# Two attention blocks on one core: eight value groups moved into the attention loop, the first maxima started among the query projections, a ring of query quarters

## The chip, the cores and the metric

The kernel runs on one core of a Trainium2 chip. TensorE (PE; its weight loads are listed apart as PEld) multiplies, VectorE (DVE) and ScalarE (ACT) read the results out of PSUM, GpSimd (POOL) works in SBUF, and SyncE (SP) issues nearly every DMA. PSUM is used as eight banks of 512 fp32 numbers per partition. The metric is the device time of one execution in microseconds (us); lower is better.

## What is computed

Two independent attention blocks, A and B, each on 2048 rows of width 640 with 32 heads of 20 columns, side by side in the output:

```python
qkv = (x @ wqkv).reshape(B, S, 3, H, Dh)              # both blocks
# A: every row sees 8 rows, 0, 2, ... 14 rows back
logits = einsum("bhsd,bhswd->bhsw", q, kg) * scale
o_a = einsum("bhsw,bhswd->bhsd", softmax(logits), vg)
# B: every row sees every row
p = softmax(einsum("bhqd,bhkd->bhqk", q, k) * scale)
o_b = einsum("bhqk,bhkd->bhqd", p, v)
return concatenate([o_a @ wo_a, o_b @ wo_b], axis=-1)
```

## The kernel before

**Products of x.** Every projection is split into a high and a low part and made of three passes (`PASSES`, L30) over five chunks of 128 rows of the width (`KC`), so one output group is 15 matmuls into one bank. The stages follow each other: A's projections (L530 on), then B's queries and keys, then B's values, then a long loop with B's attention, in which A's attention runs beside on GpSimd, then a tail.

**Queries and keys of B (L594 to L630).** 40 groups of 128 columns of weights by 512 rows of x, in ten weight chunks `MS` (keys first, queries last), two chunks `j` and four row blocks `n` at a time. Each group is copied out by ACT, its remainder is subtracted by DVE (tile `pr`), and both are stored to DRAM (`qb_d`, `kb_d`). In the last eight groups (m == 8) the weights of V's first half are loaded (tile `ww`), and the keys of the first head group (tile `bk`).

**Values of B (L922 to L977).** 32 groups (`v_group`): 16 blocks `s` of 128 rows by two halves of 320 columns; ACT copies each into a tile `ve` and SP stores it to `vb_d`. The last two (`LAG`) are left for the loop's start, so 30 stand here. B's x is held in four tiles `xn` of one rotating set of four buffers ("big"), which the keys `bk` and queries `bq` of the head groups also use; blocks 0 and 1 of x are thrown out for `bk` and `bq` of head group 0 and loaded a second time (L956) for V's last groups. V starts with blocks 2 and 3.

**Maxima.** The softmax of B subtracts each row's maximum before the exponential. The maxima are made by a pass of their own: scores are multiplied once as "m" matmuls (queries stationary, tiles `bq,bk`), and DVE reduces them from PSUM to `mx`. One of 512 such steps (`b_max`, L727) has four matmuls of 60 rows by 512 columns into two pairs of banks (`wide()`), and two DVE reductions over 1024 numbers. The maxima run 24 steps (`LEAD`) ahead of the rest: 24 `b_max` are set one behind each of V's groups 7 to 30. When 16 steps are through, `max_rows` (L636) turns the maximum round, splits it on POOL, and sends it through DRAM (`mdr`) into two extra rows of the query tile, from where the second score matmul subtracts it.

**The loop (L1008 to L1043).** 512 steps in 32 units of 16: eight head groups `g` of four heads, four quarters `qc` of the queries each. Per step: four "s" matmuls (keys stationary, tiles `bk,bq`) whose banks ACT exponentiates (tile `e`), four "m" matmuls of the step 24 ahead whose banks DVE reduces, and eight matmuls of the values (`e,vb`, "P"). The order of a unit is written out by hand:

```python
UNIT = ("P ss MM sm P sm ss MM sm sm P ss MM sm P sm MM ss sm sm P sm MM ss P sm MM ss sm sm P ss MM sm P "
        "sm MM ss sm sm P ss MM sm P sm ss MM ss G sm ss MM sm P sm MM ss P sm MM sm ss P sm MM ss P sm "
        "MM sm ss P MM MM ss P ss MM sm sm").split()          # L847
```

"ss" is a pair of score matmuls, "MM" a pair of maximum matmuls with one reduction of 1024, "sm" one of each with a reduction of 512. "G" (`group`, L1002) is one group of A's output projection (tiles `ww,aot`, 15 matmuls), and behind it the small DVE work that waited in `beside` (`flush`). `one`, `two` and `bank` choose the PSUM banks by a running account of when each was read. `b_two` (L810) issues a pair.

**Beside it.** Every fourth step calls one unit of A's attention (`a_work`), whose POOL work is on tiles `akv`; POOL also adds B's partial sums (`braw<-braw,more`) and splits A's output (`aot`). In the loop's early steps, the keys, queries (20 DMAs) and values of the next head group are loaded at every second step (`b_pieces`, L563, L1013). SP issues in program order, so a DMA that waits holds up those behind it. `after(n, ...)` defers work by n ticks; a tick is one group before the loop and one step in it.

Of the kernel before, what the change touches and what calls it, by code (L numbers as in the profile page):

```python
# [64 lines left out]
def attention_pair(ctx, tc, xa, wqk_a, wv_a, wo_a, xb, wqk_b, wv_b, wo_b, oa, ob):  # L65
# [121 lines left out]
    def columns(n):  # L187

        return (sb.tile([128, 2, KC - 1, 512], F32R, tag="big", bufs=4, name="xn"),
                sb.tile([128, 2, 1, 512], F32R, tag=f"last{n % 4 // 2}", bufs=2, name="xl"))  # L190
# [15 lines left out]
    def wide_pieces(src, second=None):  # L206

        w = [sb.tile([128, KC, 320], F32R, tag="w", bufs=4, name="ww") for _ in range(2)]
        return w, [lambda a=a, b=b: split(
            w[0][:, a:b], w[1][:, a:b], src[:, a:b], second=second, first=second and gp.tensor_copy) for a, b in PAIRS]  # L210
# [53 lines left out]
    def rows15(p, o, W):  # L264

        for k in range(KC):
            for i, (wi, xi) in enumerate(PASSES):
                pe.matmul(p[:, :320], o(xi, k), W[wi][:, k], start=(k == 0 and i == 0), stop=(k == KC - 1 and i == 2))

# [291 lines left out]
    stacks = {}  # L561

    def b_pieces(g):  # L563
        k = sb.tile([128, 2, S], F32R, tag="big", bufs=4, name="bk")
        q = sb.tile([128, NQC, 2, 512], F32R, tag="big", bufs=4, name="bq")
        v = sb.tile([128, NKB, VG], F32, tag="vb", bufs=2, name="vb")
        stacks[g] = (q, k, v)
        out = []
        hs = [slice(g * GH + 2 * r, g * GH + 2 * r + 2) for r in range(2)]

        def add(t, src, runs):
            for r0, s0, n in runs:
                out.append(lambda: sp.dma_start(t[r0:r0 + n].bitcast(F32), src[s0:s0 + n]))
        for r in range(2):
            for r0, s0, n in BK_RUNS:
                add(k[r * HALF:], kb_d[:, hs[r]], [(r0, s0, n)])
        for qc in range(NQC):
            for r in range(2):
                for r0, s0, n in BQ_RUNS:
                    add(q[r * HALF:, qc], qb_d[qc, :, hs[r]], [(r0, s0, n)])  # L580
        return out[:4], out[4:]

    def v_piece(g, b0, b1):

        sp.dma_start(stacks[g][2][:, b0:b1], vb_d[b0 * 128:b1 * 128, g * GH * VC:g * GH * VC + VG]
                     .rearrange("(b p) c -> p b c", p=128))
# [8 lines left out]
    for m in range(0, 10, 2):  # L595
        nxt = []
        for n in range(4):
            for j in range(2):
                p = next(banks)
                for k in range(KC):  # L600
                    for i, (wi, xi) in enumerate(PASSES):
                        pe.matmul(p, WB[j][:, wi, k], chunk(XB[n], xi, k), start=(k == 0 and i == 0),
                                  stop=(k == KC - 1 and i == 2))
                c = MS[m + j]
                o = (0, 1) if c < KC else (1, 0)
                pt = sb.tile([128, 2, 512], F32R, tag="p", bufs=PB, name="pr")
                act.copy(pt[:, o[0]], p)
                dve.tensor_tensor(pt[:, o[1]], p, pt[:, o[0]].bitcast(F32), ALU.subtract)
                after(1, sp.dma_start, dst_b(c, n).rearrange("t p c -> p t c"), pt.bitcast(F32))
                tick()  # L610
                if loads:
                    loads.pop(0)()
                if m < 8 and (n, j) in ((1, 0), (1, 1)):
                    w, loads = m_pieces(MS[m + 2 + len(nxt)])
                    nxt.append(w)
                elif m == 8 and (n, j) == (0, 1):
                    WV, loads = wide_pieces(wv_b[0])
                elif m == 8 and n == 3:
                    if j == 0:
                        wait[0] = 4  # L620
                        w1, more = wide_pieces(wv_b[1])
                        for fn in more:
                            fn()
                if m == 8 and n > 1:
                    if (n, j) == (2, 0):
                        k_loads, q_loads = b_pieces(0)
                    k_loads.pop(0)()
# [80 lines left out]
    def m_matmul(i, j, r, p):  # L708
# [3 lines left out]
        q, k, v = stacks[g]  # L712
# [7 lines left out]
    def max_end(i, n=2):  # L720
# [3 lines left out]
        if left_m[u] == 0:  # L724
            max_rows(*mxt[u], stacks[u // NQC][0], u % NQC)
# [15 lines left out]
    def s_matmul(i, pl, r, p):  # L741
        u, kb = divmod(i, NKB)
        g, qc = divmod(u, NQC)
        q, k, v = stacks[g]
# [26 lines left out]
    def b_pv(i):  # L771
# [15 lines left out]
        for j in range(GH):  # L787
            pe.matmul(acc[32 * j:32 * j + 32, :], stacks[g][2][:, kb, j * VC:j * VC + 32], P[i][j % 2][:, j // 2],
# [21 lines left out]
    def b_two(what):  # L810
# [39 lines left out]
        "MM sm ss P MM MM ss P ss MM sm sm").split()  # L850
    SLOT = UNIT[:UNIT.index("G")].count("P") - 1

    def b_units(pv, group):
# [5 lines left out]
        for i in range(0, NS - LEAD, NKB):  # L859
            for t in UNIT if i + NKB <= NS - LEAD else PAIR * (NKB // 4):  # L860
# [3 lines left out]
                elif t == "G":  # L864
                    group()
                elif t == "ss":
# [20 lines left out]
    def out_first(qc):  # L887

        o = columns(2)
# [32 lines left out]
    steps = iter(range(LEAD))  # L922
    WV = [WV, w1]
    groups = 0

    def v_group(n, half, s):
        p = bank()
        rows15(p, lambda xi, k: chunk(XB[n], xi, k)[:, s % 4 * 128:s % 4 * 128 + 128], WV[half])
        ve = ones[s % 4]
# [5 lines left out]


    WO, loads = [], []

    def load_out(src, W, halves=range(2)):
        for h in halves:  # L940
            w, more = wide_pieces(src[h], gp)
# [3 lines left out]
    V_GROUPS = [(n, half, s) for n in (2, 3, 0, 1) for half in range(2) for s in range(4 * n, 4 * n + 4)]  # L945
    v_late = V_GROUPS[-LAG:]
    for n, half, s in V_GROUPS[:-LAG]:
        v_group(n, half, s)
        tick()
        groups += 1  # L950
        if q_loads:
            for _ in range(4 if groups == 1 else 1):
                q_loads.pop(0)()
        if groups == 1:
            wait[0] = 5
        if groups in (8, 16):  # L956
            XB[groups // 8 - 1], more = x_pieces(xb, groups // 8 - 1, gp)
            for fn in more:
                fn()
        if groups > 6:  # L960
            for i in islice(steps, 1):
                b_max(i)
        if groups in (9, 11, 15, 17, 19, 23, 25, 28):
            next(a_work, None)
        if groups in (26, 28):
            v_piece(0, *((0, 4) if groups == 26 else (8, 16)))
        if groups == 14:
            a_turn(*done_a.pop(0)[1:])
        turn_parts()
        if groups == 28:  # L970
            wait[0] = 2
            load_out(wo_a, WO, (0,))
        if loads and groups >= 28:
# [34 lines left out]
    steps = b_units(lambda i: b_pv(i) if i >= 0 else v_group(*v_late.pop(0)), group)  # L1008
    next(steps)
    for i in range(NS + LAG):  # L1010
        g, sub = divmod(i, NQC * NKB)
        if sub == 4 and g + 1 < NG:
            k_loads, q_loads = b_pieces(g + 1)  # L1013
            for n, fn in enumerate(k_loads + q_loads + [lambda g=g + 1: v_piece(g, 0, NKB)]):
                after(1 + 2 * n, fn)
        if i in (NS - 56, NS - 40):
            out_first((i - NS + 56) // NKB)
# [9 lines left out]
        if i == 1:  # L1027
            load_out(wo_a, WO, (1,))
# [73 lines left out]
```

## Time and profile before

| what | value |
|---|---|
| three timed runs | 1774.38, 1775.05 (median), 1775.96 us |
| the profiled execution's own time | 1773.91 us, of which its span is 1772.1 us |
| TensorE's granted clock | 1.00 throughout |
| queries and keys, last eight groups | about 321.8 to 349.0 us |
| V's 30 groups with the 24 first maxima | about 349.0 to 437.1 us |
| the loop's units 0 to 31 | from 447.7 us (first accumulated sum copied out); about 39.65 us each up to unit 27 |
| units 28 and 29, with two "G" groups each | 41.88 and 41.87 us |

How to read the rows below. A line of the timeline is: start, duration, engine, line (all are L60, a helper that issues everything), operation, output<-inputs, shape, how many instructions were merged, and in brackets the idle time ahead of them with what ended it. A window's line is: stretch, its length, then the busy time of PE, PEld, DVE, ACT and POOL with the number of instructions, the granted clock, and the share and rate of the DMA engines. A line of groups is: tiles, shapes, count, total and mean duration, and idle time before.

### The profile page before, as it was taken

How to read it: one execution, taken by the hardware profiler on the slowest of the kernel's cores; microseconds unless marked ns; L12 is line 12 of the kernel's file. 1: busy time of each engine (PE TensorE's matmuls, PEld its weight loads, DVE VectorE, ACT ScalarE, POOL GpSimd, SP SyncE). 2: the span in 40 equal slices, each digit the busy share in tenths (PEclk: the TensorE clock that was granted, in tenths of full speed). 3: DMA queues.
4: the chain of work that ended last, by engine and by line, in shares of the span. 5: the costliest groups of instructions: out<-in, count | busy, mean ns of one | idle time of the engine just before them, and what ended most of it. 6: DMA issues, size and time to landing. Idle time of an engine off the chain costs nothing.

```text
span 1772.1 us, 31387 instructions
## 1 busy us (share of the span) xinstructions
PE 1761.4 (99%) x11211; PEld 982.3 (55%) x11211; DVE 1332.0 (75%) x1774; ACT 1325.7 (75%) x2593; POOL 1218.8 (69%) x1072
## 2 busy tenths in 40 slices
PE   9999999999999999999999999999999999999999
PEld 8988888888444444444444444444444444444569
DVE  3100232267999999999999999999999999999400
ACT  4222322222999999999999999999999999998981
POOL 0000058448698988989898898989898898745442
PEclk9999999999999999999999999999999999999999
DMA  6333596876443534364444435353543534222123
GB/s 230 112 98 110 175 309 244 278 227 200 121 123 114 138 103 129 115 164 113 129 114 140 119 97 149 123 144 105 156 129 93 143 103 120 87 63 62 57 70 115
DMA packets 191188, 240.20 MB, mean 136 GB/s; under 512 B 89020, under 2 KB 115260, under 8 KB 190040
## 3 DMA queue, kind: packets, MB, share of 16 engines
q1 hardware_dynamic: 190456, 237.54, 44.7%
q8 instruction: 88, 1.44, 0.3%
q14 instruction: 68, 0.56, 0.1%
q10 hardware_dynamic: 576, 0.66, 0.1%
HBM read 173.21 MB, written 64.91 MB: 134 GB/s over the span
## 4 chain that ended last, share of the span: by engine, by line
PE 86%; DVE 5%; ACT 3%; POOL 3%; DMA 1%; issue 1%; SPq 1%; POOLq 0%; DVEq 0%; ACTq 0%
PE ps_st L60 86%; DVE mx L60 5%; ACT e L60 2%; POOL akv L60 1%; ACT more L60 1%; POOL braw L60 1%; SPq L60 1%; DMA bq<-qb_d 1%; DMA stg<-wv_b 0%; ACT al L60 0%; DMA back<-tr_d 0%; POOL aot L60 0%; DMA tr_d<-turn 0%; POOL al L60 0%; POOL ao L60 0%
## 5 line engine op out<-in xcount | busy, mean ns | idle before, releaser
L60 DVE TENSOR_REDUCE mx<-ps_st 128x2 f32<-128x1024 f32 (+1 forms) x1452 | 1204.3, 901 | 53.6 <-PE ps_st L60 50.6
L60 ACT ACTIVATE e<-ps_st 128x512 f32<-128x512 f32 x2048 | 1062.2, 612 | 54.2 <-PE ps_st L60 41.7
L60 PE MATMUL ps_st<-bq,bk 62*128 62x512 f32 x2048 | 616.9, 445 | 1.4 <-ACT e L60 0.9
L60 PEld LDWEIGHTS ps_st<-bq,bk 62*128 62x128 f32 x2048 | 284.1, 184 | 492.6 <-ACT e L60 372.4
L60 PE MATMUL ps_st<-bk,bq 60*128 60x512 f32 x2048 | 551.4, 434 | 2.6 <-DMA bq<-qb_d 1.0
L60 PE MATMUL ps_st<-e,vb 128*32 128x512 f32 x4096 | 542.9, 604 | 0.2
L60 POOL TENSOR_TENSOR braw<-braw,more 128x512 f32<-128x512 f32 x224 | 288.0, 1286 | 147.9 <-ACT more L60 131.8
L60 POOL TENSOR_TENSOR akv<-akv,aq 128x1280 f32<-128x1280 f32 x64 | 188.2, 2940 | 234.8 <-DMA akv<-ka_d 234.7
L60 POOL TENSOR_TENSOR akv<-akv 128x640 f32<-128x640 f32 (+3 forms) x304 | 281.8, 927 | 23.8
L60 PEld LDWEIGHTS ps_st<-bk,bq 60*128 60x128 f32 x2048 | 257.0, 184 | 53.9 <-ACT e L60 25.2
L60 ACT COPY ro<-ps_st 128x320 f32<-128x320 f32 (+2 forms) x124 | 61.3, 496 | 198.9 <-PE ps_st L60 150.8
L60 PEld LDWEIGHTS ps_st<-e,vb 128*32 128x32 f32 x4096 | 82.0, 108 | 154.4 <-issue 74.1
L60 POOL TENSOR_TENSOR akv<-akv,al 128x1280 f32<-128x1280 f32 x64 | 152.1, 2377 | 0.2
L60 PE MATMUL ps_st<-wc,xn 128*128 128x512 f32 (+1 forms) x576 | 134.0, 378 | 0.0
L60 ACT COPY more<-ps_st 128x512 f32<-128x512 f32 x224 | 132.5, 592 | 1.8 <-PE ps_st L60 1.4
L60 PE MATMUL ps_st<-ww,xn 128*128 128x320 f32 x768 | 125.7, 314 | 0.0
L60 PEld LDWEIGHTS ps_st<-ww,xn 128*128 128x128 f32 x768 | 113.4, 188 | 20.0 <-ACT ve L60 8.4
L60 PEld LDWEIGHTS ps_st<-wc,xn 128*128 128x128 f32 x576 | 106.9, 189 | 17.6
L60 PE MATMUL ps_st<-xn,w 128*128 128x512 f32 x480 | 115.8, 390 | 0.0
L60 PEld LDWEIGHTS ps_st<-xn,w 128*128 128x128 f32 x480 | 90.1, 188 | 19.4
L60 ACT CAST pr<-ps_st 128x512 fp32r<-128x512 f32 x40 | 23.5, 587 | 101.4 <-PE ps_st L60 101.4
L60 DVE TENSOR_TENSOR pr<-ps_st,pr 128x512 fp32r<-128x512 f32 x40 | 27.7, 691 | 91.7 <-ACT pr L60 91.7
(64 smaller groups left out, 985.3 us busy)
## 6 DMA issues: line engine op xcount, KB each, us to landing
akv<-ka_d SPq DMA_DIRECT2D x128, 320.0 KB
akv<-va_d SPq DMA_DIRECT2D x128, 320.0 KB
kb_d<-pr SPq DMA_DIRECT2D x20, 512.0 KB
qb_d<-pr SPq DMA_DIRECT2D x20, 512.0 KB
bk<-kb_d SPq DMA_DIRECT2D x16, 640.0 KB
bq<-qb_d SPq DMA_DIRECT2D x64, 160.0 KB
rb<-s_d SPq DMA_DIRECT2D x128, 64.0 KB
stg<-xb SPq DMA_DIRECT2D x12, 512.0 KB
```

The source lines that it names most:

```text
L60: return self.tc.keep_in_program_order(op(*a, **k))
```

## The change

1. **Order of the last query groups and V.** The eight last query groups and V's groups stand in one list: four query groups (blocks 0 and 1 of x), V's half 0 for blocks s = 0 to 7, four query groups (blocks 2 and 3), then V's both halves for s = 8 to 15. The last two of the list are left for the loop, as before.
2. **Eight groups of V in the loop.** V's half 1 for s = 0 to 7 is made in units 1 to 8, one per unit. Those units have an order of their own, `UNIT_V`, with the same 16 "P", 64 scores and 64 maxima, but 32 "sm", 16 "ss" and 16 "MM" in place of 28, 18 and 18, and one "V" beside the "G". The block of x that a "V" needs is loaded by `x_tile` in the unit before (one DMA) and split on POOL by four instructions.
3. **Maxima.** The 24 first `b_max` are no longer set behind groups: from list position 14 (the third of the late query groups) one is issued inside the groups whenever 1.45 us of matmuls have been counted (0.227 us per query matmul, 0.147 per V matmul): after every 7 of a query group's and every 10 of V's.
4. **Memory.** The rotating set "big" becomes four fixed homes. Queries live in one ring of four quarters (home 1), loaded three units ahead, one DMA at each of the steps 1, 3, 5, 7 of a unit; keys take homes 0 and 3 in turn; A's second half of output weights takes home 2. Blocks 0 and 1 of x are not loaded a second time before the loop. V's second half of weights is split by ACT and POOL in place of ACT and DVE. The early output load of quarter 1 waits until A's output is done.

The core of the diff (the changed signatures, `big` and the home arguments are left out):

```diff
+    def b_queries(g, qc):
+        return [lambda r=r, r0=r0, s0=s0, n=n: sp.dma_start(
+            rings[0][r * HALF + r0:r * HALF + r0 + n, qc].bitcast(F32),
+            qb_d[qc, s0:s0 + n, g * GH + 2 * r:g * GH + 2 * r + 2])
+            for r in range(2) for r0, s0, n in BQ_RUNS]
...
+    UNIT_V = (
+        "sm P sm MM ss P sm ss MM sm P ss MM sm P sm sm MM sm V sm ss MM sm P sm MM ss P sm MM sm ss P sm MM "
+        "ss P sm MM sm ss P sm sm sm P sm ss MM ss G sm MM ss sm P sm MM ss P sm MM sm ss P sm sm sm P sm ss "
+        "MM sm P sm MM ss P sm MM ss").split()
+    V_UNITS = range(1, 9)
...
-            for t in UNIT if i + NKB <= NS - LEAD else PAIR * (NKB // 4):
+            for t in UNIT_V if i // NKB in V_UNITS else UNIT if i + NKB <= NS - LEAD else PAIR * (NKB // 4):
...
+    def beat(us):
+        if owed[0] is None:
+            return
+        owed[0] += us
+        if owed[0] > 1.45:
+            owed[0] = 0.0
             for i in islice(steps, 1):
                 b_max(i)
...
+    ORDER = ([("q", n, j) for n in range(2) for j in range(2)] + [("v", 0, s) for s in range(8)] +
+             [("q", n, j) for n in range(2, 4) for j in range(2)] +
+             [("v", half, s) for half in range(2) for s in range(8, 16)])
+    V_STAGE = len(ORDER) - LAG
...
+        if at in (7, 8):
+            if at == 7:
+                k_loads = b_keys(0)
+            for _ in range(2):
+                k_loads.pop(0)()
+        if at in (11, 12, 17, 19):
+            if at == 11:
+                rings.append(big(1, [128, NQC, 2, 512], "bq"))
+            for fn in b_queries(0, (11, 12, 17, 19).index(at)):
+                fn()
+        if at == 13:
+            owed[0] = 0.0
+        if at == 15:
+            WV[1], more = wide_pieces(wv_b[1], gp, first=act.copy)
...
+    def x_tile(s):
+        t = sb.tile([128, 640], F32, tag="stg", bufs=3, name="stg")
+        raw = t.rearrange("p (k c) -> p k c", c=128)
+        sp.dma_start(raw, xb[:, s * 128:(s + 1) * 128].rearrange("(k p) c -> p k c", p=128))
+        ...
+        def parts():
+            for u, r in zip(x, (raw[:, :KC - 1], raw[:, KC - 1:])):
+                gp.tensor_copy(u[:, 0], r)
+                gp.tensor_tensor(u[:, 1], r, u[:, 0].bitcast(F32), ALU.subtract)
+            xv.append((s, x))
+        after(5, parts)
+
+    def values():
+        s, x = xv.pop(0)
+        v_rows(1, s, lambda xi, k: chunk(x, xi, k), ve1)
...
+        if i >= NKB and i % NKB in (1, 3, 5, 7) and i // NKB + 3 < NG * NQC:
+            b_queries(*divmod(i // NKB + 3, NQC))[i % NKB // 2]()
+        if i % NKB == 8 and i // NKB + 1 in V_UNITS:
+            x_tile(v_loop.pop(0))
```

More of the change, by code (lines that the diff above doesn't have):

```diff
@@ L942, in load_out @@
             W.append(w)
             loads.extend(more)
[L945 to L960, printed above, removed]
+    steps = iter(range(LEAD))
```

163 lines of the change are left out of this document (87 added, 76 removed).

## The prediction

> **What bounds the kernel now.** I read the page first, for what is busy and when, then PE's timeline before the loop, then the windows of single units, then the timelines of PE and DVE around a group inside a unit.
>
> ```profile
> span 1772.1 us, 31387 instructions
> ## 1 busy us (share of the span) xinstructions
> PE 1761.4 (99%) x11211; PEld 982.3 (55%) x11211; DVE 1332.0 (75%) x1774; ACT 1325.7 (75%) x2593; POOL 1218.8 (69%) x1072
> ```
>
> PE's 99% is an envelope of pipelined matmuls, so it says nothing about which stage has room. The starts of the matmuls do. Here is the end of the query stage, V's groups without maxima, and the first two with them:
>
> ```profile
> 342.14 2.91 PE L60 MATMUL ps_st<-xn,w 128*128 128x512 f32 x12
> 344.88 0.86 PE L60 MATMUL ps_st<-xl,w 128*128 128x512 f32 x3
> 345.58 2.91 PE L60 MATMUL ps_st<-xn,w 128*128 128x512 f32 x12
> ...
> 360.00 1.92 PE L60 MATMUL ps_st<-ww,xn 128*128 128x320 f32 x12
> 361.75 0.60 PE L60 MATMUL ps_st<-ww,xl 128*128 128x320 f32 x3
> 362.19 1.92 PE L60 MATMUL ps_st<-ww,xn 128*128 128x320 f32 x12
> 363.94 0.60 PE L60 MATMUL ps_st<-ww,xl 128*128 128x320 f32 x3
> 365.19 0.47 PE L60 MATMUL ps_st<-bk,bq 60*128 60x512 f32 x1 [0.64 <-DMA bq<-qb_d]
> 366.04 0.73 PE L60 MATMUL ps_st<-bk,bq 60*128 60x512 f32 x3 [0.39 <-DMA bq<-qb_d]
> 366.70 2.03 PE L60 MATMUL ps_st<-ww,xn 128*128 128x320 f32 x12
> 368.57 0.60 PE L60 MATMUL ps_st<-ww,xl 128*128 128x320 f32 x3
> 369.10 0.73 PE L60 MATMUL ps_st<-bk,bq 60*128 60x512 f32 x4
> ```
>
> From start to start a query group takes 345.58 - 342.14 = 3.44 us, a V group 362.19 - 360.00 = 2.19, and a V group with one maximum step 369.10 - 366.04 = 3.06; a step of maxima thus costs PE 3.06 - 2.19 = 0.87 us. PE is the bound here, and DVE has room: its two reductions of one step, in the same stage, with the idle time ahead of them:
>
> ```profile
> 375.76 2.36 DVE L60 TENSOR_REDUCE mx<-ps_st 128x2 f32<-128x1024 f32 x2 [0.70 <-PE ps_st L60]
> ```
>
> In the loop it is the other way round. Windows of unit 4, unit 5 and unit 28 (columns: PE, PEld, DVE, ACT, POOL busy):
>
> ```profile
> 606.46:646.25 39.79, 39.57 (x273) 17.09 (x275) 38.65 (x51) 37.42 (x76) 34.08 (x30) 1.00 0.55 153
> 646.25:685.80 39.55, 39.54 (x273) 17.12 (x274) 39.24 (x56) 37.15 (x75) 37.38 (x34) 1.00 0.45 125
> 1559.80:1601.68 41.88, 41.72 (x288) 19.37 (x290) 39.05 (x55) 37.63 (x75) 20.19 (x20) 1.00 0.23 62
> ```
>
> DVE is busy 38.65 of 39.79 and 39.24 of 39.55 us: it has 1.14 and 0.31 us to spare, 0.73 on average. ACT has 2.4. What PE has to spare must be worked out from its steps. Unit 4 around its "G":
>
> ```profile
> 617.52 1.07 PE L60 MATMUL ps_st<-e,vb 128*32 128x512 f32 x8
> 618.52 0.50 PE L60 MATMUL ps_st<-bq,bk 62*128 62x512 f32 x2
> 618.86 0.40 PE L60 MATMUL ps_st<-bk,bq 60*128 60x512 f32 x2
> 619.10 0.40 PE L60 MATMUL ps_st<-bq,bk 62*128 62x512 f32 x1
> 619.10 0.39 PE L60 MATMUL ps_st<-bk,bq 60*128 60x512 f32 x1
> 619.42 1.06 PE L60 MATMUL ps_st<-e,vb 128*32 128x512 f32 x8
> ...
> 621.24 0.51 PE L60 MATMUL ps_st<-bq,bk 62*128 62x512 f32 x2
> 621.84 2.44 PE L60 MATMUL ps_st<-ww,aot 128*128 128x320 f32 x15
> 624.21 0.50 PE L60 MATMUL ps_st<-bq,bk 62*128 62x512 f32 x1
> ```
>
> This step had no wait: "P" 1.00 us, the pair behind it 0.34, an inner pair 0.24, the pair ahead of the next "P" 0.32. A unit has 16 "P" and 64 pairs: 16 x (1.00 + 0.34 + 0.32) + 32 x 0.24 = 34.2, and the group 624.21 - 621.84 = 2.37 makes 36.6 us. So PE waits for banks some 3.1 of the mean 39.67 us of a unit. Into this balance, with eight banks between the engines, the eight groups go.
>
> **What leaves the stages before the loop.** PE executes the same query groups, the same 24 steps of maxima at 0.87 us, and eight V groups fewer: 8 x 2.19 = 17.5 us off the path, since PE is the bound there.
>
> The first maxima ran into a late load, which the chain of waits shows as one piece (start, duration):
>
> ```profile
> 355.63 10.37 DMA bq<-qb_d
> ```
>
> The queries landed at 366.0: the four matmuls that should have followed the group of 362.19 were held so that the next group started at 366.70 in place of 362.19 + 3.06 = 365.25, a stall of 1.45 us. In the new order the keys are asked for behind list position 7, about 4 x 3.44 + 4 x 2.19 = 22.5 us into the list, the first queries behind position 11 (31.3 us in), and the first maximum comes two query groups and seven matmuls later, 8.4 us after. That is less than the 10.37 us of before, but those stood behind more loads: the keys had been asked for only in the last four query groups, and the second half of V's weights, which now comes later, lay between them. I take the stall as gone, -1.45; if the queries still come late it is back, up to 1.45.
>
> **What the denser maxima cost.** From position 14 on PE has 2 x 3.44 + 14 x 2.19 = 37.5 us of groups and 24 x 0.87 = 20.9 of maxima, 58.4 in all. Counting 0.227 and 0.147 us per matmul to 1.45, the 24 steps just fit: the sixteenth falls into position 23, the last near the start of position 29. DVE needs 24 x 2.36 = 56.6 for them. One step every ten V matmuls is 10 / 15 x 2.19 + 0.87 = 2.33 us of PE against 2.36 of DVE: DVE becomes the pace, by a hair. To its load come the remainders of two query groups and the small work that it did in V's stage anyway (A's softmax, the first turn of maxima; an estimate of 1.3, twice the 0.62 of a row quoted further down):
>
> ```profile
> L60 DVE TENSOR_REDUCE mx<-ps_st 128x2 f32<-128x1024 f32 x596 | 718.5, 1217 | 27.7 <-PE ps_st L60 26.8
> L60 DVE TENSOR_REDUCE mx<-ps_st 128x1 f32<-128x512 f32 x856 | 553.0, 681 | 25.9 <-PE ps_st L60 23.8
> L60 DVE TENSOR_TENSOR pr<-ps_st,pr 128x512 fp32r<-128x512 f32 x40 | 27.7, 691 | 91.7 <-ACT pr L60 91.7
> ```
>
> 2 x 0.69 + 1.3 + 24 x 0.03 = 3.4 us, of which PE's lead of one step of maxima buffers about 1: I take +2.4, between 0 (all of it buffered) and 4. The maximum of unit 0 is complete in position 23, its rows are asked for four ticks later, two groups (7 us) ahead of the loop's first scores: no wait. V's second half of weights is split on POOL now, five positions before use; the splits of x that stood on POOL in this stage are gone, so POOL has no more to do. Sum before the loop: -17.5 - 1.45 + 2.4 = -16.5 us.
>
> **What a "V" costs a unit.** Three bounds. PE: 36.6 + 2.37 = 39.0 us, so the group fits below 39.67 if its waits fall from 3.1 to 0.7; if none of them falls the unit grows by 2.37 and the pair's longer wait ahead of a group, 0.3 (621.84 follows a pair that began at 621.24, against the usual 0.32): 2.67. Unit 28 is the nearest row: its second group, set right behind the first, cost 41.88 - 39.67 = 2.2 us. DVE: four pairs of halves are reduced singly that were reduced together: two reductions of 1024 become four of 512, 2 x (2 x 0.681 - 1.217) = 0.29 us. And there is a hole while PE is in the group. At the "G" of unit 4:
>
> ```profile
> 621.66 1.22 DVE L60 TENSOR_REDUCE mx<-ps_st 128x2 f32<-128x1024 f32 x1
> 622.79 0.62 DVE L60 TENSOR_REDUCE am<-al 128x32 f32<-128x256 f32 x1
> ...
> 624.77 1.82 DVE L60 TENSOR_REDUCE mx<-ps_st 128x1 f32<-128x512 f32 x2 [0.87 <-PE ps_st L60]
> ```
>
> From 622.79 to 624.77, 1.98 us, no bank of maxima is ready; `flush` fills 1.1 of it with small work and 0.87 is idle. At a "V" there is no `flush`. But "MM sm V" gives DVE one half more ahead than "MM ss G": the hole is about 1.98 - 0.68 = 1.30 us. With 0.29 that is 1.59 if DVE cannot use its idle 0.73 anywhere, 0.86 if it can use all of it. I take 1.1, two thirds of it used: 8 x 1.1 = +8.8 us; bounds 0.29 (no hole) and 2.67, times eight +2.3 and +21.4.
>
> The Trainium skill ("Perfetto Trace Analysis", Identifying the Most-Contended Engine) judges TensorE's room by the share of its weight loads and not by its busy time, and takes the fullest other engine for the bound. Here the loads fill 17.1 of 39.79 us; by that rule PE has room for many groups, V would cost only DVE's extra 0.29, and the whole would come to 1773.91 - 16.5 + 2.3. The steps above disagree with the rule as far as a hand-made order goes: 34.2 us of a unit are fixed spacings between pairs and "P", though loads fill less than half.
>
> **Beside the path.** ACT copies one group more, well inside its 2.4 us. POOL gets four instructions per unit of V:
>
> ```profile
> L60 POOL TENSOR_TENSOR xn<-stg,xn 128x512 fp32r<-128x512 f32 x16 | 20.9, 1306 | 1.3
> ```
>
> That one, its copy (at most the same) and two of a quarter of the size: below 3.3 us. POOL is busy 34.08 and 37.38 us; two units hold 71.5 + 6.6 of 79.3. It hides, with a lag of a microsecond in odd units. Were POOL late, the split maximum would be late, but this has slack:
>
> ```profile
> L60 SPq DMA_DIRECT2D bq<-mdr x4: 248/254/256, 632.9 to 672.4; - x4
> ```
>
> The rows go out at 632.9 and 672.4, the next units begin at 646.25 and 685.80: 13 us. SP issues as many query loads as before, only later; the slot that each overwrites was last read a unit earlier. The x of eight blocks is as many bytes as the second load it replaces. The early output load of quarter 1 moves by a step or two, with some ten steps to its use. All at 0.
>
> **The sum.** Against the profiled execution: 1773.91 - 16.5 + 8.8 = 1766.2 us. The median of the runs shown is 1.1 above it, so the forecast for a median is 1775.05 - 7.7 = 1767.3.
>
> **The rivals.**
> *V is free (0.18).* DVE keeps all its idle time for the hole and no bank is missed: -16.5 + 2.3 = -14.2, 1760.8. For it: ACT's 2.4 and PE's 3.1 us of waits. Against it: DVE is 99% busy in odd units, and every "G" leaves a hole. This is also what the skill's rule of the last part but one would give.
> *PE is full (0.14).* Its waits do not shrink, since they come from the banks' rhythm; each "V" costs 2.2 to 2.67 us: -16.5 + 17.6 to 21.4 = +1.1 to +4.9, 1776.2 to 1780.0. For it: unit 28 paid 2.2. Against it: there both groups stood together, and DVE starved once for a long time in place of twice for a short one. It decides against the change from 16.5 / 8 = 2.06 us per unit.
> *The maxima keep their period (0.05).* In V's stage PE's steps of maxima start at 369.10 + 3 x 3.06 = 378.28, which is 0.16 us after DVE's reductions ended (375.76 + 2.36 = 378.12). If that is a dependence and not chance, no step can follow in less than 3.06 us: 24 x 3.06 = 73.4 against 58.4 + 2.4, +12.6, so +4.9 and 1780.0. Against it: DVE idles 0.70 in the period shown, two pairs of banks alternate, and a V group with no maxima gives 2.19, and two pairs of maxima alone explain the 0.87 (a pair takes 0.24 to 0.34 in the loop, and the change to and from the group some more).
> *The groups move but something queues (0.05).* A late x or ring load stalls some units: around 1770.
>
> **How the numbers follow.** The forecast's case (0.58) runs from 0.75 to 1.5 us per "V", with the 0 to 4 us of DVE's pace: 1763 to 1772. The range reaches down to the free V with little lost to DVE's pace, 1759, and up to the weak end of a full PE, 1776. A difference of 0.2% is 3.55 us, about what a measurement of this kernel can tell from no change. Faster by more: the forecast but for its upper end, the free V, and half of the small queueing case, 0.78; slower by more: the strong half of the full PE and the maxima's period, 0.09; the rest, 0.13, within.
>
> **What would show it.** V's first matmul in the loop in unit 1; the first copy of a summed value in the loop, at 447.7 before, near 431.2. In the stage before, reductions of 1024 back to back on DVE at 1.18 us with little idle time, and PE's steps of maxima waiting for DVE, for a few us in all. Units 1 to 8 near 40.8 us, a DVE hole of about 1.3 us at each "V", units 9 to 27 unchanged at 39.65. It is wrong if those units stand at 41.7 and above, if the loop starts later than 435, or if later units have grown.

## The result and the profile after

The changed kernel takes 1790.31 us (median of 7 runs, 1782.27 to 1794.74) against 1774.93 us before (7 runs, 1773.33 to 1778.5). The ratio of the means of these runs is 1.0076, 95% interval 1.0055 to 1.0097 (the medians alone would give 1.0087). It is slower where the prediction said faster, and outside its range. One run below, of e_b_addr, took 2268.61 us at a mean granted clock of 0.654 and is left out of the ratios. The profiled execution took 1785.71 us; its page begins:

```profile
span 1783.9 us, 31518 instructions
PE 1766.7 (99%) x11211; PEld 985.3 (55%) x11211; DVE 1335.2 (75%) x1787; ACT 1323.6 (74%) x2587; POOL 1231.7 (69%) x1102
```

PE executes exactly as many matmuls as before, 11211, so the 11.8 us of span are waiting and slower work. Stage by stage, profile against profile:

| stretch | before, us | after, us | difference | predicted |
|---|---|---|---|---|
| start to the first late query group | 321.66 | 325.40 | +3.7 | 0 |
| from there to the loop's first score matmul | 117.82 | 109.26 | -8.6 | -16.5 |
| first score to the end of unit 0 | 47.96 | 48.22 | +0.3 | 0 |
| units 1 to 8 | 317.45 | 332.29 | +14.8 | +8.8 |
| units 9 to 29 | 838.65 | 837.86 | -0.8 | 0 |
| units 30, 31 and the tail | 128.54 | 130.86 | +2.3 | 0 |

The stage boundaries are matmul starts of PE and ACT's first copy of each unit's sum. Nearly half of the expected gain ahead of the loop is missing, and each unit with a "V" is 1.85 us longer in place of 1.1.

PE's timeline where the first maximum meets the queries, as in the rows of before around 365.19:

```profile
363.78 1.80 PE L60 MATMUL ps_st<-xn,w 128*128 128x512 f32 x7
367.75 0.50 PE L60 MATMUL ps_st<-bk,bq 60*128 60x512 f32 x1 [2.17 <-DMA bq<-qb_d]
368.72 0.70 PE L60 MATMUL ps_st<-bk,bq 60*128 60x512 f32 x3 [0.47 <-issue]
369.35 1.86 PE L60 MATMUL ps_st<-xn,w 128*128 128x512 f32 x5
371.00 1.06 PE L60 MATMUL ps_st<-xl,w 128*128 128x512 f32 x2
371.99 1.22 PE L60 MATMUL ps_st<-bk,bq 60*128 60x512 f32 x4
```

The stall that was to vanish has grown from 1.03 to 2.64 us, and behind it four matmuls of the maxima take 1.22 us in place of 0.73. Two windows of the same stage say why, and how full the engines are afterwards (PE, PEld, DVE, ACT, POOL busy; the third number from the end is the granted clock):

```profile
370.10:373.50 3.40, 3.40 (x10) 1.86 (x9) 2.15 (x3) 0.00 (x0) 0.00 (x0) 0.50 0.64 244
...
380.21:428.48 48.27, 47.31 (x268) 35.09 (x267) 45.75 (x44) 6.88 (x16) 35.83 (x28) 1.00 0.70 212
```

For 3.4 us TensorE ran at half its clock, which costs 1.7. Before, the clock was 1.00 throughout. From 380.21 to 428.48 stand 19 steps of maxima, 2.54 us each, with DVE busy for 95% of it.

The chain of waits ahead of that stall (start, duration):

```profile
349.44 10.50 DMA bk<-kb_d
...
359.96 7.75 DMA bq<-qb_d
```

One of the queries' loads was issued when a load of the keys landed. SP's own rows show how they were held:

```profile
349.07 0.70 SPq L60 DMA_DIRECT2D bk<-kb_d  x2
351.28 0.87 SPq L60 DMA_DIRECT2D bk<-kb_d  x2
...
357.89 6.17 SPq L60 DMA_DIRECT2D bq<-qb_d  x4
```

Four query loads, issued in one go before (353.33 to 355.9), now spread over 6.17 us: 357.89, 359.96, 360.30 and 363.79. SP's loads use eight semaphores in turn, and here a load is issued only when the one eight before it has landed. The keys' four loads, issued from 349.07 to 352.16, landed at 356.10, 359.94, 363.78 and 365.48, so the second and the fourth query load each waited for one of them (359.94 and 363.78). An estimate of what this hold costs: the matmuls wanted the queries at 365.6; had the second load been issued right behind the first, at about 358.3, and taken its 7.75 us, it would have landed at about 366.0 in place of 367.71.

The loop. Units 1 to 8 take 41.34, 41.54, 41.16, 42.67, 41.17, 41.45, 41.17 and 41.79 us. Windows of units 4 and 5 after:

```profile
606.93:649.61 42.68, 41.10 (x288) 19.34 (x290) 39.38 (x53) 38.20 (x77) 37.17 (x32) 1.00 0.58 156
649.61:690.77 41.16, 40.93 (x288) 19.54 (x288) 39.84 (x58) 37.92 (x75) 39.35 (x40) 1.00 0.42 119
```

In unit 5 DVE is busy 0.60 us longer than in the unit 5 of before, and idle for 1.32 us in place of 0.31: together the 1.61 by which the unit grew. DVE at the "V":

```profile
647.53 5.53 DVE L60 TENSOR_REDUCE mx<-ps_st 128x1 f32<-128x512 f32 x7
653.77 2.42 DVE L60 TENSOR_REDUCE mx<-ps_st 128x1 f32<-128x512 f32 x3 [0.71 <-PE ps_st L60]
```

The hole is 0.71 us, not 1.30; the rest of the idle time is small and elsewhere in the unit. In unit 4 there is more. PE and then SP around 640:

```profile
641.90 0.49 PE L60 MATMUL ps_st<-bq,bk 62*128 62x512 f32 x1 [1.25 <-DMA bq<-mdr]
```

```profile
627.97 0.38 SPq L60 DMA_DIRECT2D s_d<-sm  x1
633.52 1.71 SPq L60 DMA_DIRECT2D rb<-s_d  x4
635.33 2.64 SPq L60 DMA_DIRECT2D mdr<-mtr  x4
...
639.25 0.57 SPq L60 DMA_DIRECT2D bq<-mdr  x2
```

PE waits for the maximum's rows. On SP they stand behind the broadcast of the normalisation (`rb`), which here waited 5.2 us for its own data to land; the loads of the rows were issued at 639.25 and landed at 641.9, after the unit's scores wanted them at 640.65.

### The profile page after: what moved, and what is told of

It reads as the page before. It is cut to its first block, busy times and chain, and to the rows that moved or that the text cites. A ratio compares the mean times of both kernels' runs of the same rounds, so it can differ in the third digit from the quotient of the medians.

```text
span 1783.9 us, 31518 instructions
## 1 busy us (share of the span) xinstructions
PE 1766.7 (99%) x11211; PEld 985.3 (55%) x11211; DVE 1335.2 (75%) x1787; ACT 1323.6 (74%) x2587; POOL 1231.7 (69%) x1102
## 4 chain that ended last, share of the span: by engine, by line
PE 90%; DVE 3%; DMA 2%; POOL 2%; ACT 2%; issue 1%; SPq 0%; DVEq 0%; POOLq 0%; ACTq 0%
PE ps_st L60 90%; DVE mx L60 3%; ACT e L60 1%; POOL braw L60 1%; DMA bk<-kb_d 1%; POOL akv L60 1%; DMA bq<-mdr 0%; DMA bq<-qb_d 0%; SPq L60 0%; ACT more L60 0%; DMA mdr<-mtr 0%; POOL xn L60 0%; DMA stg<-xa 0%; ACT al L60 0%; POOL al L60 0%
## 5 line engine op out<-in xcount | busy, mean ns | idle before, releaser
L60 DVE TENSOR_REDUCE mx<-ps_st 128x1 f32<-128x512 f32 (+1 forms) x1468 | 1209.2, 895 | 49.8 <-PE ps_st L60 44.2
L60 PEld LDWEIGHTS ps_st<-bk,bq 60*128 60x128 f32 x2048 | 262.4, 184 | 55.5 <-ACT e L60 18.8
L60 PEld LDWEIGHTS ps_st<-ww,xn 128*128 128x128 f32 x768 | 114.3, 188 | 18.8 <-issue 7.9
```

The lines of the kernel that those rows point to most:

```text
L60: return self.tc.keep_in_program_order(op(*a, **k))
```

## The experiments

Twelve kernels, each run beside the kernel before on the same chip, whose median there is 1773.88, 1773.97 or 1775.39 us. Two of them, e_order and e_plain_v, have a single run. Only the telling part of each edit is shown; "..." stands for what is left out.

**c_before: the kernel before again.**

> The kernel before, once more, as a control with its own trace and the granted clock of every run. Theory: the projection matmuls of 512 columns keep their median spacing of 227 ns (the changed kernel has 229 to 232), the granted clock stays at 1.00 in nearly all runs, and the median is within 0.1% of 1775 us. Rival (chip and not kernel): spacings of 230 ns or more and clocks of 0.995 to 0.999 show up here as well.

1774.02 us (11 runs), ratio 1.0000 (0.9991 to 1.0009). 0.2% is measurable, and the losses below are the change's own. Here the first maxima waited 0.46 us, so even the 1.03 of the profile shown above varies.

**e_no_v: the eight groups left out.**

```diff
-    V_UNITS = range(1, 9)
+    V_UNITS = ()
...
```

> The changed kernel without the eight V groups in the loop: all units have the old order, no x is loaded or split for them (these eight groups of values are left out, ones are stored in their place). Theory: units 1 to 8 fall from 41.2 to 42.7 us back to 39.65, so that the time is about 15 us below the changed kernel's (profile near 1771); the loop still starts near 434 us, and the slow start of the maxima stays. Rival (the units are slowed by the ring's loads or the memory layout, not by the groups): they stay above 41.

1772.61 us, ratio 0.9991 (0.9982 to 1.0000). Units 1 to 8 are back at 317.28 us, so the ring, the four homes and the queries' loads cost the units nothing. But 17.5 us of PE work less make the kernel only 0.1% faster: the loss ahead of the loop does not come from "V". The first score stands at 437.44, 2 us earlier than before, behind a wait of 3.61 us for the queries and two windows of half clock.

**e_order: the new order of units, its "V" empty.**

```diff
                 elif t == "V":
-                    values()
+                    pass
...
```

> The changed kernel with the new order in units 1 to 8 but nothing done at a V (the eight groups of values are left out, no x is loaded; ones are stored in their place). Theory: of the 1.65 us that a V costs a unit, 0.3 to 0.6 comes from the order itself, with four more single reductions on DVE: odd units at 39.8 to 40.1 us. Rival A (the order costs all of it): 41.2. Rival B (the order costs nothing): 39.55.

1781.16 us (one run). Units 1 to 8 take 325.09 us, 0.96 each above before, without one matmul of V in them. Its units 4 and 5:

```profile
606.05:646.61 40.56, 39.68 (x273) 17.13 (x273) 39.14 (x53) 37.86 (x75) 33.71 (x30) 1.00 0.57 156
646.61:687.16 40.55, 39.80 (x273) 17.23 (x274) 39.85 (x58) 37.82 (x75) 37.76 (x34) 1.00 0.39 115
```

PE's busy time is that of before (39.57 and 39.54) within 0.3 us; DVE has 0.5 to 0.6 us more work and idles 1.42 and 0.70 where it idled 1.14 and 0.31. The order alone, with the loads and splits of x left out too, costs more than half of what a "V" costs.

**e_plain_v: the old order with a "V" put in.**

```diff
+    UNIT_V = list(UNIT)
+    UNIT_V.insert([n for n, t in enumerate(UNIT) if t == "P"][4] - 2, "V")
```

> The changed kernel with the old order in units 1 to 8 and a V put between two pairs ahead of the fifth P. Theory: DVE's and ACT's hole is what a V costs, and the old order has fewer banks full ahead of it: units 1 to 8 at 41.4 to 41.9 us, a little worse than the new order's 41.17 and 41.45. Rival (the new order is the trouble): 40.5 or less.

1796.15 us (one run); every unit from 1 to 8 takes 42.45 to 42.49 us, 2.8 above before. Unit 5:

```profile
656.08:698.54 42.46, 42.38 (x288) 19.09 (x289) 39.68 (x56) 37.98 (x75) 39.68 (x41) 1.00 0.42 117
```

Set into the old order at this one place, the group costs its full 2.37 us and 0.4 more: nothing of PE's waits shrinks. Another place was not tried. With the order written for it the same group comes to 1.65 (below), against 0.96 for that order with no group in it.

**e_one_x: one block of x loaded and split, used eight times.**

```diff
...
-        if i % NKB == 8 and i // NKB + 1 in V_UNITS:
-            x_tile(v_loop.pop(0))
+        if i == 8:
+            x_tile(0)
```

> The changed kernel with the block of x for the loop's V groups loaded and split once only, and used eight times (seven blocks of values are wrong by that). Theory: the price of a V is PE's group and the hole it leaves on DVE and ACT, so odd units stay at 41.17 us; only units 4 and 8, which waited for a late row of maxima, lose 1.2 and 0.3: 1.5 to 2.5 us less in all. Rival (the price is POOL's four extra instructions and SP's extra load): the units fall to about 40 us, 10 us or more less in all.

1789.45 us, ratio 1.0081 (1.0067 to 1.0096), like the change itself. Odd units are at 41.09 to 41.33, 0.1 lower at most; units 2, 4 and 8 at 42.47, 43.18 and 43.35 are not helped. Neither the loads of x nor POOL's splits are the price, and POOL's split is not what made the rows late, though the chain of waits in unit 4 runs through it.

**e_later: the maxima begin 2 us later and stand closer among the queries** (after every 6 matmuls in place of 7; among V's groups 0.147 us a matmul gives every 10 as before).

```diff
-        if owed[0] > 1.45:
+        if owed[0] > 1.36:
...
-            owed[0] = 0.0
+            owed[0] = -2.0
```

> The changed kernel with the first step of maxima one half of a query group later (3.4 us into list position 14 in place of 1.6) and the steps slightly denser behind it. Theory: the wait of 2.9 us for the first queries falls below 1, no stretch of half clock follows it, and the loop's first pair starts 2 to 4 us earlier than 434.66. Rival 1 (DVE alone sets the stage's length, the wait costs nothing): the loop starts no earlier. Rival 2 (the half clock has nothing to do with the wait): a stretch of half clock is still found near 370 us.

1786.74 us, ratio 1.0068 (1.0056 to 1.0081). The wait for the queries falls to 0.84 + 0.49 us and no half clock follows it. The first score comes 1.1 us earlier than in the changed kernel. From its second step on, DVE ends what waits the steps have (0.18 to 0.34 us): the closer steps among the queries run into DVE. Unit 4 grew to 44.61 here, with a wait of 1.62 us for the maximum's rows and a half clock of its own at 642.3.

**e_keys: the keys' loads asked for one position earlier.**

```diff
-        if at in (7, 8):
-            if at == 7:
+        if at in (6, 7):
+            if at == 6:
...
```

(with one query group moved behind the fourth V group to make room, and one more piece of V's weights split ahead of the list)

> The changed kernel with the keys of the first head group asked for one list position, 3.4 us, earlier (the fourth query group stands behind the first four V groups, so that the first block of x is free sooner); the rest as it is. Theory: the first queries wait on SP behind the keys, whose transfers take 11 to 13 us; with the keys earlier the queries land by 365.5 us, the first maximum waits under 0.5 us (2.2 and 0.5 before), no half clock follows near 370, and the loop's first score comes 3 to 5 us earlier than 434.66. Rival (DVE's pace alone sets the stage's length): it comes less than 1 us earlier.

1787.72 us, ratio 1.0076 (1.0056 to 1.0096). A miss: the keys were issued from 345.9 to 351.08, little earlier at their end, the query loads were still held by them (issued 358.17 to 365.38), and PE still waited, so that no run shows the stage with the hold gone:

```profile
368.15 0.50 PE L60 MATMUL ps_st<-bk,bq 60*128 60x512 f32 x1 [2.26 <-DMA bq<-qb_d]
```

**e_layout: the changed kernel with the four homes side by side,** at the four SBUF addresses that they had before, two of them exchanged.

```diff
...
+    early.update({n: big(n, [128, 2, KC - 1, 512], "xn") for n in range(4)})
     XA = [columns(0)]
```

> The changed kernel with its four homes reserved ahead of everything else, so that the tiles of x, the staging tiles and the query pieces lie at the addresses that they had before (the change had moved them; no instruction is changed). Theory: the spacing of the 512-column projection matmuls falls from a median of 230 ns to 227, the first query or key matmul comes at 212.2 us in place of 214.3, the first V group some 3.9 us earlier than 339.2, and the time falls by 4 us. Rival (the spacing follows from the longer program or from the chip): it stays at 230, and nothing is gained.

1785.63 us, ratio 1.0064 (1.0048 to 1.0081). The first V group starts at 335.13 in place of 339.19: 4.06 us back, by addresses alone. More than half of it is lost again by the first score (432.83 against 434.66), because the queries do not come as much earlier:

```profile
364.69 0.64 PE L60 MATMUL ps_st<-bk,bq 60*128 60x512 f32 x1 [3.29 <-DMA bq<-qb_d]
```

and 6.8 us of half clock follow, twice as long as in the changed kernel.

**e_b_addr: the kernel before with the addresses of after,** nothing else changed.

```diff
+    def big(shape, name):
+        return sb.tile(shape, F32R, tag=f"big{turns.pop(0)}", bufs=1, name=name)
...
-        return (sb.tile([128, 2, KC - 1, 512], F32R, tag="big", bufs=4, name="xn"),
+        return (big([128, 2, KC - 1, 512], "xn"),
...
```

> The kernel before, its program unchanged, with its four big buffers and all that lies behind them at the SBUF addresses of the kernel after. If the addresses slow the 512-column matmuls: spacing 230 to 232 ns in the projections in place of 227, first query group 2 us later, start of the late query list 4 us later (325.4 in place of 321.5), time 1778 (+0.2%). Rival, the slowing comes from the new order, its loads or its placing of work: spacing 227, time 1774 as before.

1779.0 us (8 runs; 1778.74 without the one of 2268.61), ratio 1.0026 (1.0016 to 1.0037). Third query group, in c_before and then here:

```profile
218.52 2.88 PE L60 MATMUL ps_st<-xn,w 128*128 128x512 f32 x12
221.24 0.84 PE L60 MATMUL ps_st<-xl,w 128*128 128x512 f32 x3
221.92 2.88 PE L60 MATMUL ps_st<-xn,w 128*128 128x512 f32 x12
```

```profile
221.10 2.95 PE L60 MATMUL ps_st<-xn,w 128*128 128x512 f32 x12
223.89 0.86 PE L60 MATMUL ps_st<-xl,w 128*128 128x512 f32 x3
224.58 2.96 PE L60 MATMUL ps_st<-xn,w 128*128 128x512 f32 x12
```

From start to start the group takes 3.40 us there and 3.48 here. The groups of queries and keys follow the block of x that they read, in both kernels (the addresses are those that the build of each kernel gives its tiles): block 0, which did not move (64128 bytes into the partition), 3.40 to 3.43; block 1 3.40 at byte 113280 and 3.49 at 133120; blocks 2 and 3 3.41 to 3.44 at 96896 and 80512 and 3.50 at 149504 and 174080. The first V group starts 4.7 us later, with nothing added, moved or waited for. The loop's units are the same to 0.05 us over units 1 to 8.

**e_b_wait: the kernel before with its first maximum one V group earlier.**

```diff
-        if groups > 6:
+        if groups > 5:
```

> The kernel before with the first maximum one group of V earlier, so that PE runs into the late queries 2.2 us sooner and waits about 2.9 us in place of 1.03. If a long wait of PE brings a window of half clock: a window of 3.4 us at 0.5 directly behind the wait, and 2.2 + 1.7 = 3.9 us more, 1778. Rival, the windows in the other runs came from something else in the new order: clock 1.00 throughout, 2.2 us more at most, 1776.

1780.44 us, ratio 1.0033 (1.0020 to 1.0046). PE's timeline, then the window behind the wait:

```profile
364.63 2.08 PE L60 MATMUL ps_st<-bk,bq 60*128 60x512 f32 x4 [2.80 <-DMA bq<-qb_d]
366.64 3.57 PE L60 MATMUL ps_st<-ww,xn 128*128 128x320 f32 x12
```

```profile
364.30:371.10 6.80, 6.37 (x21) 4.91 (x21) 2.36 (x2) 0.67 (x3) 0.00 (x0) 0.50 0.58 192
```

Only the place of the maxima was changed, and with the longer wait came the half clock, for two windows of 3.4 us where I had expected one. The loop starts 5.2 us later than in c_before: some 2.3 of wait and 3.4 of clock, less what the early step gives back.

**e_both: the addresses of before and the later, closer maxima together.**

> The kernel after with the addresses of before and the later, closer maxima, the two edits that each took away one loss ahead of the loop. If these losses are independent: spacing 227, wait for the first queries under 1.4 us, no half clock near 365 to 375, first score near 430, and 1781 to 1782 (still 0.4% slower than before). Rival, the queries only come as late against the earlier list: wait over 2 us, half clock behind it, 1785 as with the addresses alone.

1783.39 us, ratio 1.0052 (1.0037 to 1.0067). Ahead of the loop the two losses do add up: the wait is short and the clock stays at 1.00,

```profile
363.95 0.50 PE L60 MATMUL ps_st<-bk,bq 60*128 60x512 f32 x1 [1.02 <-DMA qb_d<-pr]
```

and the first score stands at 428.49, 9.9 us ahead of c_before. But in its profile unit 4 took 47.43 us (PE, then its window):

```profile
637.57 0.79 PE L60 MATMUL ps_st<-bq,bk 62*128 62x512 f32 x1 [3.09 <-DMA bq<-mdr]
```

```profile
637.20:644.00 6.80, 6.43 (x26) 1.92 (x28) 2.52 (x3) 2.54 (x5) 5.17 (x7) 0.50 0.51 164
```

The late rows of the maximum stop PE for 3.09 us, and two windows of half clock follow.

**e_rows: as e_both, with the broadcast of the normalisation one step later,** so that on SP the maximum's rows go first.

```diff
-            after(2, bcast)
-            after(4, pool, raw, raw, rb, ALU.mult)
+            after(3, bcast)
+            after(5, pool, raw, raw, rb, ALU.mult)
```

> The same with the broadcast of the normalisation one step later, so that on SP the maximum's rows go out ahead of it. If the broadcast's wait for its data holds the rows in units 2, 4 and 8: those units come down from 42 to 43.4 to about 41.3, units 1 to 8 to about 330.5, time 2 to 3 us below the run with the two edits, near 1779. Rival, the rows are late on POOL or in landing: units 2, 4 and 8 as before, no gain.

SP in unit 4, then units 4 and 5:

```profile
623.55 0.38 SPq L60 DMA_DIRECT2D s_d<-sm  x1
624.02 1.81 SPq L60 DMA_DIRECT2D mdr<-mtr  x4
...
629.84 1.77 SPq L60 DMA_DIRECT2D rb<-s_d  x4
631.71 0.54 SPq L60 DMA_DIRECT2D bq<-mdr  x2
```

```profile
602.51:643.91 41.40, 41.06 (x288) 19.57 (x290) 39.27 (x53) 38.13 (x76) 37.57 (x32) 1.00 0.60 161
643.91:685.11 41.20, 40.98 (x288) 19.52 (x290) 39.94 (x58) 37.93 (x75) 39.39 (x41) 1.00 0.43 121
```

Units 2, 4 and 8 are at 41.40 to 41.46, units 1 to 8 at 330.64, as expected: the broadcast held the rows. Clean of late rows, a "V" costs (330.64 - 317.43) / 8 = 1.65 us. The time is 1781.87 us, ratio 1.0044 (1.0027 to 1.0061); its interval and that of e_both overlap, so the gain of the whole is not shown. In its profile the first maxima waited 1.83 us (one window of half clock), and unit 26, outside the change, took 44.93 us with another at 1520.5, behind a wait of 3.21 us for DVE, which itself had stood 3.91 us behind POOL; whether the later broadcast caused that was not tried. With three of its losses repaired, the change is still slower than the kernel before.

## Why the prediction was wrong

The gap between predicted and measured is 19.5 us in the profiled executions (11.8 - (-7.7)). The terms below make 4.3 + 3.4 + 3.7 + 6.0 + 2.3 = 19.7; unit 0 and units 9 to 29 give back 0.5, and 0.2 were lost in the list ahead of position 14. The medians lie further apart, 23.0 us (1790.31 against 1767.3); the profiled execution was one of the faster ones, and what the others lost beyond it has no profile.

**What leaves the list: right as PE's own work.** Eight groups at 2.19 us did leave it. "PE is the bound there" held only until the maxima stood closer: even in e_both, with the addresses repaired and the stall down to 1.5 us, 9.9 of the 17.5 us arrive at the loop.

**"I take the stall as gone": wrong, about 4.3 us.** I compared how long after the request the queries were needed (8.4 us) with how long one load had taken (10.37) and argued the difference away with fewer loads ahead. I did not count that a load on SP waits for the one eight before it. The keys' loads, close ahead, took 7 to 14 us, and held the query loads. The wait is 2.64 us and the half clock behind it costs 1.7. That the hold makes most of the wait is read from SP's rows (some 1.7 us by the estimate above); that the wait costs this time e_later and e_b_wait show.

**Nothing said of the clock.** The page of before showed 1.00 throughout, and I priced a wait at its length. The runs show that it can cost more than twice that. Ahead of the first maxima, waits of 0.5 to 1.5 us brought no half clock (c_before, e_later, e_both); 1.83 + 0.49 (e_rows), 2.17 + 0.47 and 2.83 + 0.68 (e_order) brought one window of 3.4 us; 2.80 in e_b_wait and 3.29 + 0.35 in e_layout brought two. The length of the wait alone does not decide it; the traces show what does better. In every trace the clock changes on a grid of 3.413 us: in the twelve with a half clock before the end, the first stands behind a whole number of such windows, 105 to 486, at full clock. Ahead of the tail there are twelve falls to half clock, and each follows a window of that grid in which TensorE was busy for 56% or less by the profile; behind windows at full clock with 62% and more none follows. Two such windows of the changed kernel, the one with the stall's end and the one with unit 4's wait of 1.25 us (55% and 63% busy):

```profile
366.70:370.10 3.40, 1.88 (x7) 1.15 (x8) 0.88 (x1) 0.00 (x0) 0.00 (x0) 1.00 0.93 299
639.80:643.20 3.40, 2.15 (x16) 0.82 (x14) 2.82 (x4) 2.81 (x6) 3.40 (x2) 1.00 0.96 299
```

Half clock follows the first and not the second. It lasted a second window in the six cases in which TensorE was busy for 52 to 90% of the first one, and ended after one in the six in which TensorE was busy throughout it. This is read from the traces; e_b_wait alone was made to bring a window about. So the same wait can cost more or less by where it falls on the grid. The Trainium skill ("TensorE: Matmul & The Clock Gate", Part 1) states a half rate, a free-running window of 3413 ns, and a fall to half rate after at least one idle window. The length, the rate and the grid agree with the trace; that a whole idle window of some 3.4 us is needed does not, since waits of 2.3 to 2.8 us in all, in windows busy up to 56%, did it here. In the other runs of the changed kernel, 1782.27 to 1794.74, the mean clock falls from 1.000 to 0.995 as the time grows, which fits more such windows; they have no profile.

**"What the denser maxima cost, +2.4": too small by some 3 us.** From position 14 (363.78) to the first score (434.66) are 70.9 us. The prediction's 58.4 + 2.4, with 2.4 for the V group that stands between the list and the first score, make 63.2; stall and half clock are 4.3; 3.4 are left. I had the row (2.36 us of reductions per step) and then let PE's lead buffer 1 us of DVE's other work; over 24 steps no lead is left. The rest is hand-over, which the sum put at nothing: in the 48.27 us shown above DVE works for 45.75 and is idle for 2.5, 2.1 of them waiting for PE's scores, while PE's weight loads and matmuls wait 5.0 us for DVE. So DVE sets the pace, with a hole of its own. This is read from the trace; no run took work off DVE in this stage. e_later shows only that steps set closer among the queries wait for DVE.

**Addresses: a term that was missing, +3.7.** I read "four fixed homes" as a renaming. It moved three of the four blocks of x and the small tiles `xl`, and e_b_addr shows the same slowing in the kernel before.

**"What a V costs, 1.1": 1.65, and 1.85 with the late rows, 6.0 us in all.** The step that failed is the split into 0.29 of reductions and a hole of which "two thirds" would be taken up by idle time. The 0.29 is about what the instructions give; unit 5's groups of reductions, before and after:

```profile
L60 DVE TENSOR_REDUCE mx<-ps_st 128x2 f32<-128x1024 f32 x18 | 21.7, 1217 | 0.0
L60 DVE TENSOR_REDUCE mx<-ps_st 128x1 f32<-128x512 f32 x29 | 18.8, 681 | 0.3 <-PE ps_st L60 0.2
```

```profile
L60 DVE TENSOR_REDUCE mx<-ps_st 128x1 f32<-128x512 f32 x33 | 21.5, 685 | 1.2 <-PE ps_st L60 1.1
L60 DVE TENSOR_REDUCE mx<-ps_st 128x2 f32<-128x1024 f32 x16 | 19.5, 1217 | 0.1
```

18.8 + 21.7 = 40.5 of durations became 41.0; what they add to DVE's busy time is 0.6. But the idle time did not shrink, it grew by 1.0. DVE, busy 97 to 99% of a unit, had no idle time to lend here, and the new order brought holes of its own: 0.96 of the 1.65 are there with no group in them (e_order), and the rest, 0.69, comes with the group. The hole at the "V" was smaller than I said (0.71), so the price was not where I looked for it. The rival "PE is full", 2.2 to 2.67, is what the old order gives (2.8 in e_plain_v); the order removes part of it. The rule of the Trainium skill that the prediction weighed ("Perfetto Trace Analysis", Identifying the Most-Contended Engine: room by the share of weight loads; the page names the share of peak FLOPs beside it, which was not worked out) would have given 0.29; e_plain_v with 2.8 and e_rows with 1.65 contradict that.

**"Beside the path, all at 0": right for POOL and x, wrong for the maximum's rows.** e_one_x bears out the first. The 13 us of slack were counted from the issue on SP to the next unit; landing and the scores that run ahead of the unit's first copy (the rows were wanted at 640.65, unit 5 begins at 649.61) left less, and 5.2 us of the broadcast's wait used it up in units 2, 4 and 8: 1.7 us in the changed kernel's profile, 6 in that of e_both.

**The tail, +2.3, of which 1.7 is a window of half clock** at 1667. In e_b_addr one stands at 1663.1 behind the same short waits (0.38 and 0.48 us) as in c_before, which has none; e_both has the longer wait of the changed kernel (1.24) and none. What starts it there stays open.

What was named as telling came out so: the loop started later than 435 (first copy at 442.93), units 1 to 8 averaged 41.54 us, just short of the 41.7 named, and units 9 to 29 did not grow.

## What to carry to other kernels

Work taken off one engine is worth its duration only until the next engine sets the pace: eight groups off PE bought at most 10 us of 17.5, and in the stage that they left DVE's maxima then took 95% of the time. Put into a hand-ordered loop that is 99% full on another engine, a group brings the price of the new order with it, so time that order empty before filling it. And where a change moves buffers, or lets TensorE wait for about 2 us, look at the spacing of untouched matmuls and at the granted clock first: both losses lie outside the lines that were edited.

## What the runs showed of the hardware

The spacing of 512-column matmuls in the projections depended on where x lay in SBUF, the same in two kernels with different orders: 3.40 us per group of 15 with x (`xn`) at byte 64128, 3.49 to 3.50 at 133120, 149504 and 174080. At 80512, 96896 and 113280 a group took 3.40 to 3.44, and there e_layout, which exchanged two blocks, tells `xn` from the small `xl` beside it: 80512 had 3.44 in the kernel before and 3.40 in e_layout, 113280 the reverse, while both times the group was fast with `xl` at 133760 and slow with `xl` at 186368.

Matmul by matmul one pattern fits both tiles in all four layouts (before, after, e_b_addr, e_layout), in A's projections, where x is the stationary operand, as in B's. Where the tile of x begins at a multiple of 256 bytes (the three slow addresses above, and `xl` at 165888, 169984, 182272 and 186368), matmuls are 233 to 235 ns apart on average, and some of the next six are still slow. Where it begins 128 bytes past such a multiple, as all the weights do (the other addresses, and `xl` at 129664 and 133760), they are 227 ns apart. That 133120 is slow and 133760 fast rules out that the higher part of the memory is slow as such. One `xl`, at 84608, only ever follows slow matmuls and tells little. The pattern was not tried by moving one tile by 128 bytes, and what is behind it stays open.

The Trainium skill ("SBUF — State Buffer", Who interferes with whom) says that PE never waits on anyone there; it speaks of other engines and has no word on addresses, and no run here showed who, if anyone, was in the way.

TensorE's half clock came in pieces of 3.413 us on a fixed grid, behind a window of that grid in which TensorE was busy for 56% or less; in the tail pieces also stood behind windows busy for 61 to 75%, while other windows with 65 to 75% there had none behind them. Loads of the keys, 640 and 352 KB, took 7 to 14 us to land, and a query load behind them 7.75 us; with eight semaphores in turn, such a load stopped SP's queue for everything behind it.
